# Forward and backward of two SSM-convolution and MLP layers on one core: order of the loads for the last products, storing of the shift gradient, and the last output block in two column halves

## The chip, the cores and the metric

The kernel runs on 1 core of one Trainium2 chip. The metric is device time in microseconds (us); lower is better. A core has TensorE (PE, whose weight loads the profile lists apart as PEld), VectorE (DVE), ScalarE (ACT), GpSimd (POOL) and SyncE (SP); SP, ACT and POOL also issue DMAs.

## The reference

Four residual blocks are applied to x = A_q [1, 2048, 448] (S = 2048 rows, D = 448 columns): block A, block B, block A, block B, each on the layer norm of its input. The outputs are the result and the gradients of eight inputs for a given `grad_out`.

```python
def _A_ref(q, k, v, shift_k, ssm_k, ssm_D):
    k_shift = sum(k_pad[:, t:t+S, :] * shift_k[:, ks-1-t] for t in range(ks))   # ks = 4
    kv = k_shift * v
    y = irfft(rfft(kv, 2*S) * rfft(ssm_k, 2*S))[:S] + kv * ssm_D   # along S
    return q * y
def _B_ref(x, w1, w2):
    return silu(x @ w1) @ w2                                       # 448 -> 1792 -> 448
x = A_q
for f in (_A_ref, _B_ref, _A_ref, _B_ref):
    x = x + f(_layernorm(x), ...)
```

Two of the outputs matter here. Output 7 is the gradient of `w1` [448, 1792]: a sum over the 2048 rows, and over the two B layers, of (normed input) transposed times (gradient at the 1792 columns). Output 4 is the gradient of `A_shift_k` [448, 4].

## The kernel before, in words

The kernel writes its instructions through a small planner. Each call of `Sched.op` (L168) records an operation with a cost per engine that may run it, a priority, and what it reads and writes. `Sched.plan` (L243) then plays the program with these costs and fixes an order for each engine, which buffer of a ring each tile gets, and, where two engines could do an operation, which one does. A DMA's landing is planned from the table `RATE` (L140): "plain", "turn", "load" (transposing loads) and "rows" (stores in short rows). `behind` holds an operation back until others have been issued; `after` until they are done. `emit` (L338) writes the instructions out in the planned order. So a changed cost or `behind` can change the order on every engine from that place on.

The program has three stages: `Head` (the convolution spectra and the first forward product), `Flow` (16 row tiles, each through all blocks forward and backward), and `Tail` (weight gradients and the gradients of block A). The change is in `Tail`:

- `fft`, `chunk` (L848 to L935) take the gradient of `kv` through the Fourier products.
- `ends` (L959) turns the spectra back (`ps_gkv` L980, `ps_gK` L1002) and makes the gradients of v, k, `ssm_k`, `ssm_D` and `shift_k`. For `shift_k`, columns are taken in bands of 32, four bands to a group `q` (groups 0 to 2 have 128 columns, group 3 has 64). TensorE multiplies the bands (`ps_sk`, L1051) in two halves `h` of 8 row tiles; VectorE's `pick` (L1058) takes the diagonals out, sums them (`gsk`, L1063) and writes four columns of `gskb` (L1065), one row for each of the group's columns. After all four groups, TensorE turns the 16 columns of `gskb` into rows (`row4`, L1071 and L1075, PSUM tile `ps_gs`), ScalarE copies the 1 x 1792 result (`gsr`, L1079), and one POOL DMA stores it (L1080).
- `jobs` (L1082) is called for "w2" and for "w1". A job `p` (7 of them, `NF // 2`) makes 256 of the 1792 rows of a weight gradient: two blocks `u` of 128, each a sum of 32 matmuls 128 x 128 by 128 x 448 (L1172): 16 row tiles `t` for each of two groups `gi`, one per B layer. The stationary operand comes from `jb`, a tile of 128 x 16 x 256 brought for each (p, gi) by `bring` (L1107). In the w1 jobs `jb` is brought by a transposing DMA (L1112) from DRAM (`GH1` for gi = 0, `GH0` for gi = 1); its buffers are three of ring `jb`, and `Minv`'s space for every fourth one. The moving operand of the w1 jobs is `nmov` (L1090): two tiles 128 x 16 x 448, `nm[1]` for gi = 0 and `nm[0]` for gi = 1, each loaded by two plain DMAs of 896 KB (L1095). All these loads are issued by SP, in the order that the planner fixed: both loads of `nm[1]`, the last `jb` of the w2 jobs, the transposing load for (0, 0), both loads of `nm[0]` (which are `behind` that load), the transposing load for (1, 0), then (0, 1), (1, 1) and on.
- The order on TensorE in the first two w1 jobs is laid down by hand (L1157, L1174): job 0 with gi = 0 (32 matmuls), job 1 with gi = 0 (32), job 0 with gi = 1, job 1 with gi = 1. The two blocks of job 1 share one PSUM tile of two banks (`pair`, L1150). The `ps_sk` matmuls of the last `shift_k` groups are placed between them.
- A finished block is copied from PSUM to `dob` (L1188, on ScalarE or VectorE by `_copy`, L90, which shows as L92 or L94). For jobs 0 to 5 an SP transposing DMA (L1191) turns `dob` into `do`, and four POOL DMAs store it (L1208, L1210). For the last job TensorE turns `dob` (`ps_dt`, four transposes of 112 columns to a block, L1197), ScalarE or VectorE copies that into `do` (L1200), and one SP DMA stores it (L1212).

```python
            for i in (1, 0):
                for h in range(2):
                    ...
                    s.op({"SP": 0.4}, lambda e, i=i, hs=hs: nc.sync.dma_start(out=nm[i][:, hs, :], in_=_pm(k.N_d[i][:])[:, hs, :]),
                         ..., behind=k.loads[-1 - i:][:1])
...
            for p, gi, at in ((0, 0, pr), (1, 0, pr + 0.2), (0, 1, pr + 1), (1, 1, pr + 2)):
                bring(p, gi, 0, 16, at)
```

Of the kernel before, what the change touches and what calls it, by code (L numbers as in the profile page):

```python
# [12 lines left out]
FP32 = mybir.dt.float32  # L13
BF16 = mybir.dt.bfloat16
ACT = mybir.ActivationFunctionType
# [5 lines left out]
P = 128  # L21
S = 2048
D = 448
# [4 lines left out]
ND = 4  # L28
# [61 lines left out]
def _copy(nc, eng, out, in_):  # L90
    if eng is nc.scalar:
        nc.scalar.copy(out, in_)  # L92
    else:
        eng.tensor_copy(out, in_)  # L94
# [38 lines left out]
class Sched:  # L133
# [3 lines left out]
    AHEAD = 0.2  # L137
    SHARED = 3.0
    STEP = 20
    RATE = {"plain": 300e3, "turn": 160e3, "load": 190e3, "rows": 220e3}  # L140

    def __init__(self, k, bufs, opener, start):
        self.k = k
# [16 lines left out]
    def at(self, base, *key):  # L160
        return base + NUDGE.get(key, 0.0)
# [188 lines left out]
def _pm(ap2d):  # L350
    return ap2d.rearrange("(p j) d -> p j d", j=J)
# [487 lines left out]
class Tail:  # L839
# [119 lines left out]
    def ends(self, pr):  # L959
# [63 lines left out]
        for g in range(8):  # L1023
# [13 lines left out]

            adds.append(s.op({"DVE": 2.9}, add, r=[x for x in prods], w=[a0, a1, gk], prio=pr + 5))
            s.op({"POOL": 0.6}, lambda e, gk=gk, g=g: nc.gpsimd.dma_start(out=out2[:, 2 * g:2 * g + 2, :], in_=gk[:]), r=[gk], prio=pr + 5, dma=("plain", 230e3))
        gskb = s.vb("P2", "gskb", [P, 4, 4], BF16, "gskb")  # L1040
        prev = []
        for q in range(4):
            nb = 4 if q < 3 else 2
            pd = self.unit([P, 4, 32], FP32, "ps_sk")
            for h in range(2):

                def ms_(e, q=q, h=h, nb=nb, pd=pd):
                    for sl_ in range(8 * h, 8 * h + 8):
                        for b in range(nb):
                            c0 = 32 * (4 * q + b)  # L1050
                            nc.tensor.matmul(pd[32 * b:32 * b + 32, :, :], lhsT=gks[:, sl_, c0:c0 + 32], rhs=kx[:, sl_:sl_ + 4, c0:c0 + 32],  # L1051
                                             start=(sl_ == 0), stop=(sl_ == 15), tile_position=(0, 32 * b))

                prev = [s.op({"PE": 1.1}, ms_, r=[*gs, kx], w=[pd], prio=pr + 4, after=[*prev, adds[2 * q + h]])]
            sel = s.vb("P2", "sel", [P, 4, 32], FP32, "gsel")
            gsk = s.vb("P2", "gsk", [P, 4], FP32, "gsk")

            def pick(e, q=q, nb=nb, pd=pd, sel=sel, gsk=gsk):  # L1058
                for b in range(nb):
                    m = k.ident[32 * b:32 * b + 32, 32 * b:32 * b + 32].unsqueeze(1)  # L1060
                    nc.vector.tensor_tensor(out=sel[32 * b:32 * b + 32], in0=pd[32 * b:32 * b + 32], in1=m.to_broadcast([32, 4, 32]), op=ALU.mult)
                n = 32 * nb
                nc.vector.tensor_reduce(out=gsk[0:n], in_=sel[0:n], axis=mybir.AxisListType.X, op=ALU.add)  # L1063
                for j in range(4):
                    nc.vector.tensor_copy(gskb[0:n, q, j:j + 1], gsk[0:n, 3 - j:4 - j])  # L1065

            s.op({"DVE": 1.5}, pick, r=[pd], w=[sel, gsk, gskb], prio=pr + 4)

        pg = self.unit([1, 4, D], BF16, "ps_gs")

        def row4(e):  # L1071
            for q in range(4):
                n = 128 if q < 3 else 64
                for j in range(4):
                    nc.tensor.transpose(pg[0:1, j, 128 * q:128 * q + n], gskb[0:n, q, j:j + 1], k.ident[0:n, 0:n])  # L1075

        s.op({"PE": 1.0}, row4, r=[gskb], w=[pg], prio=pr + 4)
        gsr = s.vb("P2", "gK", [1, D * 4], BF16, "gsr")
        s.op({"ACT": 1.8}, lambda e: nc.scalar.copy(gsr[:].rearrange("o (d j) -> o j d", j=4), pg[:]), r=[pg], w=[gsr], prio=pr + 4)  # L1079
        s.op({"POOL": 0.6}, lambda e: nc.gpsimd.dma_start(out=k.outs[4].rearrange("(o d) j -> o (d j)", o=1), in_=gsr[:]), r=[gsr], prio=pr + 4, dma=("plain", 5e3))  # L1080

    def jobs(self, which, pr):  # L1082
        nc, s, k = self.nc, self.s, self.k
        if which == "w2":
            gm = s.vb("res", "W1", [P, NT, D], BF16, "gmov")
            gs = [gm.sub() for _ in range(4)]
            gl = [lambda i=i: s.op({"SP": 0.4}, lambda e: nc.sync.dma_start(out=gm[:, 4 * i:4 * i + 4, :], in_=_pm(k.grad_out[0])[:, 4 * i:4 * i + 4, :]), w=[gs[i]], prio=pr - 30, dma=("plain", 458e3), behind=[k.lastA_op]) for i in range(4)]
            groups = [("A1", [gs[t // 4] for t in range(NT)], lambda t: gm[:, t, :]), ("A0", k.G2v, lambda t: k.G2[:, t, :])]
        else:
            nm = [s.vb("PF", ("A1", "B1v")[i], [P, NT, D], BF16, "nmov") for i in range(2)]  # L1090
            nh = [[v.sub() for _ in range(2)] for v in nm]
            for i in (1, 0):
                for h in range(2):
                    hs = slice(8 * h, 8 * h + 8)
                    s.op({"SP": 0.4}, lambda e, i=i, hs=hs: nc.sync.dma_start(out=nm[i][:, hs, :], in_=_pm(k.N_d[i][:])[:, hs, :]),  # L1095
                         r=[k.st_[("n", i, j)] for j in range(8 * h, 8 * h + 8)], w=[nh[i][h]], after=self.done[i], prio=pr - 30 if i else pr + 0.5, dma=("plain", 917e3), behind=k.loads[-1 - i:][:1])
            groups = [("GH1", [nh[1][t // 8] for t in range(NT)], lambda t: nm[1][:, t, :]), ("GH0", [nh[0][t // 8] for t in range(NT)], lambda t: nm[0][:, t, :])]
        out7 = k.outs[7].rearrange("(c p) f -> p c f", p=DC)
        prev = []
# [21 lines left out]
        if which == "w2":  # L1121
            bring(0, 1, 0, 16)
            for x in gl:
                x()
            for a in ((0, 0, 0, 15), (1, 1, 0, 16), (1, 0, 0, 15)):
                bring(*a)
        else:
            for p, gi, at in ((0, 0, pr), (1, 0, pr + 0.2), (0, 1, pr + 1), (1, 1, pr + 2)):
                bring(p, gi, 0, 16, at)
        for p in range(NF // 2):  # L1130
            q = s.at(pr + 12.5 * p, p, which)
            early = p < 2
# [26 lines left out]
            both = True  # L1159
            steps = [(u, gi) for gi in range(2) for u in range(2)] if both else [(u, gi) for u in range(2) for gi in range(2)]  # L1160
            if split is None:
                split = [(u, gi, range(8 * h, 8 * h + 8)) for u, gi in steps for h in range(2)]
            mine = []
            for x, (u, gi, ts) in enumerate(split):
                ends = [[y for y in range(len(split)) if split[y][0] == u][z] for z in (0, -1)]
# [4 lines left out]
                def mm(e, ts=ts, gi=gi, u=u, rows=rows, ps=pss[u], at=groups[gi][2], first=(x == ends[0]), last=(x == ends[1])):  # L1170
                    for t in ts:
                        nc.tensor.matmul(ps[:, :D], lhsT=rows(t, gi, u), rhs=at(t), start=(first and t == ts[0]), stop=(last and t == ts[-1]))  # L1172

                if (which, p, x) == ("w1", 1, 4):  # L1174
                    prev = [first[-1], mine[-1]]
                prev = [s.op({"PE": 0.19 * len(ts)}, mm, r=[*[parts[gi][t] or k.lastA for t in ts], *[groups[gi][1][t] for t in ts]], w=[pss[u]], prio=q + 0.05 * x - (12.35 if (which, p) == ("w1", 1) and x < 4 else 0), after=prev + (self.last if p else [k.lastG] if u and which == "w2" else []))]
# [5 lines left out]
            for u in range(2):  # L1182
                ps = pss[u]
# [4 lines left out]
                s.op({"ACT": 0.55, "DVE": 0.62}, lambda e, ps=ps, ob=ob: _copy(nc, e, ob[:], ps[:, :D]), r=[ps], w=[ob], prio=q)  # L1188
# [4 lines left out]
                pt = self.unit([DC, ND, P], BF16, "ps_dt")  # L1193

                def tr(e, ob=ob, pt=pt):
                    for dc in range(ND):
                        nc.tensor.transpose(pt[:, dc, :], ob[:, dc * DC:(dc + 1) * DC], k.ident[:])  # L1197

                s.op({"PE": 0.25}, tr, r=[ob], w=[pt], prio=q)
                s.op({"ACT": 0.6, "DVE": 0.4}, lambda e, pt=pt, o=o, u=u: _copy(nc, e, o[:, :, u, :], pt[:]), r=[pt], w=[o], prio=q)  # L1200
# [14 lines left out]
def kernel(  # L1215
# [66 lines left out]
               u=3, cp=6, junk=1, cc=6, tt=1, G3=2, gy2=3, G1=1, gy=1, gq=2),  # L1282
    "PF": dict(A1=1, Minv=1, B1v=1, gks=1, kx=1),
    "P1": dict(pq=3, sp=1),
    "P2": dict(skb=1, gK=2, gkv=2, gKD=1, sel=2, gsk=2, gskb=1, gKr=1, oo=2, ob=2),
}


# [98 lines left out]
```

## Time and profile before

| | us |
|---|---|
| median of 3 runs | 701.48 (700.76 to 703.49) |
| the profiled execution: its own time | 699.83 |
| its span, first to last instruction | 698.0 |
| TensorE busy | 676.8 |
| VectorE busy | 512.8 |
| ScalarE busy | 401.8 |
| GpSimd busy | 168.2 |
| first matmul of the w1 jobs, from the span's start | 601.53 |

Times in views are us from the start of the span. Busy matmul times overlap a little, since a matmul's end is modelled with the pipeline behind it; the spacing of matmuls is read from the starts of the runs that follow each other. "x32" is a run of 32 like instructions; what stands in brackets is idle time before it, and what ended it. The DMA view gives, per kind of issue, the count, the size and the time from issue to landing.

### The profile page before, as it was taken

The numbers are of one execution on the slowest core, as the hardware profiler recorded it, in microseconds if no ns is written. First come the engines' busy times: TensorE is split into PE (matmuls) and PEld (weight loads), VectorE is DVE, ScalarE is ACT, GpSimd is POOL, SyncE is SP. The second block draws the span as 40 slices with busy tenths as digits, with TensorE's granted clock in tenths as the row PEclk, the third lists the DMA queues.
The fourth block names the chain that finished last, engine by engine and source line by source line (L and its number), as shares of the span: only waits on it lengthen the run. The fifth ranks groups of instructions, "written<-read, shape, count | busy, mean of one in ns | idle before, by whom it ended". The sixth has DMA issues, their size and how long they took to land. (4 is left out here: it accounts for less than half of the span.)

```text
span 698.0 us, 18012 instructions
## 1 busy us (share of the span) xinstructions
PE 676.8 (97%) x7448; PEld 469.2 (67%) x7464; DVE 512.8 (73%) x1203; ACT 401.8 (58%) x486; POOL 168.2 (24%) x290
## 2 busy tenths in 40 slices
PE   6999898999999999999999999999999999999997
PEld 4887666776767776777767767655767765455553
DVE  5989798668889888888889877864699679951000
ACT  4989987776667556766567666425876550002001
POOL 1254153203222323122212201013143131102221
PEclk9999999999999999999999999999999999999999
DMA  9979988989788978787886769977699679999972
GB/s 320 289 247 291 363 165 181 199 180 190 181 154 180 183 189 181 177 176 187 183 181 143 174 158 237 296 191 231 201 387 350 181 258 302 302 238 219 230 159 46
DMA packets 280671, 151.86 MB, mean 218 GB/s; under 512 B 230159, under 2 KB 261631, under 8 KB 280205
## 3 DMA queue, kind: packets, MB, share of 16 engines
q1 hardware_dynamic: 265854, 108.29, 67.2%
q0 software_dynamic: 13968, 41.62, 19.5%
q8 instruction: 58, 0.95, 0.6%
q10 hardware_dynamic: 766, 0.80, 0.4%
q14 instruction: 25, 0.20, 0.1%
HBM read 50.68 MB, written 54.60 MB: 151 GB/s over the span
## 5 line engine op out<-in xcount | busy, mean ns | idle before, releaser
L1172 PEld LDWEIGHTS <-jb 128*128 128x128 bf16 x892 | 85.8, 98 | 81.6 <-DMA jb<-GH_d 2.0
L92 ACT CAST ghp<-ps_g 128x896 bf16<-128x896 f32 x64 | 58.1, 908 | 58.5 <-PE ps_g L672 48.5
L726 PE MATMUL ps_o<-w2sb,aT 128*128 128x448 bf16 x448 | 89.7, 352 | 0.8 <-ACT aT L700 0.8
L726 PE MATMUL ps_n<-w1T,ghT 128*128 128x448 bf16 x448 | 90.0, 352 | 0.0
L1172 PE MATMUL ps_d<-nmov,jb 128*128 128x448 bf16 x448 | 86.3, 353 | 2.2 <-DMA jb<-GH_d 1.6
L663 PE MATMUL ps_h<-nT,w1sb 128*128 128x128 bf16 x1344 | 85.6, 219 | 0.8 <-ACT nT L92 0.8
L663 PE MATMUL ps_g<-nT,w2T 128*128 128x128 bf16 x1344 | 85.7, 219 | 0.0
L663 PEld LDWEIGHTS <-w2T 128*128 128x128 bf16 x1344 | 77.3, 98 | 7.2
L663 PEld LDWEIGHTS <-w1sb 128*128 128x128 bf16 x1344 | 76.7, 98 | 5.2 <-issue 0.9
L726 PEld LDWEIGHTS <-aT 128*128 128x128 bf16 x448 | 43.0, 98 | 38.4 <-ACT aT L700 1.0
L726 PEld LDWEIGHTS <-ghT 128*128 128x128 bf16 x448 | 43.1, 98 | 37.8
L700 ACT ACTIVATE aT<-ps_h 128x896 bf16<-128x896 f32 x64 | 56.7, 916 | 19.9 <-PE ps_h L672 11.0
L622 POOL TENSOR_TENSOR rstd<-ve,mhalf 128x1 f32<-128x1 f32 x64 | 39.3, 614 | 106.6 <-DVE ve L619 106.6
L700 ACT ACTIVATE dT<-ps_h 128x896 bf16<-128x896 f32 x60 | 53.3, 915 | 14.9 <-PE ps_h L672 10.0
L750 DVE SCALAR_TENSOR_TENSOR junk<-u,n 128x448 bf16<-128x448 bf16 x64 | 39.9, 624 | 23.2 <-ACT u L829 22.2
L92 ACT CAST dob<-ps_d 128x448 bf16<-128x448 f32 x13 | 6.9, 532 | 70.9 <-PE ps_d L1172 70.9
L700 ACT ACT_TABLE_LOAD x36 | 46.2, 1283 | 1.2 <-issue 0.6
L1172 PE MATMUL ps_d<-G,jb 128*128 128x448 bf16 x224 | 45.7, 353 | 0.1
L1172 PE MATMUL ps_d<-gmov,jb 128*128 128x448 bf16 x220 | 45.1, 352 | 0.0
L617 DVE BATCH_NORM_STATS2 st<-x 128x6 f32<-128x448 bf16 x64 | 40.0, 625 | 1.5
L739 DVE TENSOR_TENSOR ghT<-ghp,dT 128x896 bf16<-128x896 bf16 x64 | 39.4, 620 | 1.1 <-ACT ghp L92 0.9
L829 ACT ACTIVATE u<-ps_n,rstd 128x448 bf16<-128x448 f32 x32 | 20.3, 636 | 32.3 <-POOL rstd L622 13.8
(180 smaller groups left out, 1218.2 us busy)
## 6 DMA issues: line engine op xcount, KB each, us to landing
A_d<-turned SPq DMA_DIRECT2D x32, 448.0 KB, 4.0
GH_d<-ghT SPq DMA_DIRECT2D x32, 448.0 KB, 4.1
jb<-A_d SPq DMA_DIRECT2D x12, 1024.0 KB, 6.7
KK<-KK POOLq DMA_DIRECT2D x14, 256.0 KB, 5.1
spec_K<-KK POOLq DMA_DIRECT2D x7, 512.0 KB, 6.0
spec_KV<-X POOLq DMA_DIRECT2D x7, 512.0 KB, 7.7
N_d<-n POOLq DMA_DIRECT2D x32, 112.0 KB, 4.0
sp_c<-spec_KV POOLq DMA_DIRECT2D x14, 256.0 KB, 6.6
```

The costliest lines, as they stand in the source:

```text
L92: nc.scalar.copy(out, in_)
L617: nc.vector.bn_stats(out=st[:], in_=x[:])
L622: s.op({"POOL": 1.0}, lambda e: nc.gpsimd.tensor_tensor(out=rs[:], in0=ve[:], in1=self.k.mhalf[:, 0:1], op=ALU.pow), r=[ve], w=[rs], prio=pr)
L663: nc.tensor.matmul(ps[:, i, :], lhsT=at(b, ft), rhs=nT[:, b, :], **f)
L700: prev = [s.op({"ACT": 0.93}, lambda e, i=i, fun=fun, out=out, late=late: nc.scalar.activation(out[:, 7 * i:7 * i + 7, :], c[:, 7 * i:7 * ...
L726: nc.tensor.matmul(po[:, :D], lhsT=a[:, ft, :], rhs=wt[:, ft * D:(ft + 1) * D], start=(ft == 0), stop=(ft == NF - 1))
L739: s.op({"DVE": 0.57}, lambda e, i=i, t=t: nc.vector.tensor_tensor(out=gh[:, 7 * i:7 * i + 7, :], in0=t[:], in1=d[:, 7 * i:7 * i + 7, :], o ...
L750: nc.vector.scalar_tensor_tensor(out=junk[:], in0=u[:], scalar=1.0, in1=n[:], op0=ALU.mult, op1=ALU.mult, accum_out=cp[:, 1:2])
L829: s.op({"ACT": 0.85}, lambda e: nc.scalar.activation(u[:], pn[:, :D], ACT.Identity, scale=r[:], accum_out=cp[:, 0:1]), r=[pn, r], w=[u, cp ...
L1172: nc.tensor.matmul(ps[:, :D], lhsT=rows(t, gi, u), rhs=at(t), start=(first and t == ts[0]), stop=(last and t == ts[-1]))
```

## The change

Three edits in `Tail`, and one number of the planner:

1. The loads of `nm[0]` move: they are recorded behind the second transposing load, (1, 0), instead of the first, (0, 0).
2. The gradient of `shift_k` is no longer turned on TensorE. Each group `q` has a small tile `gskb` [128, 4] of its own (4 buffers), and one POOL DMA a group stores its 128 (or 64) rows of 4 elements to output 4. `row4`, the copy `gsr` and its store are gone.
3. In the last w1 job block u = 1 is computed in two column halves (224 columns each) with a PSUM tile each; copying, turning and copying out of that block go by halves.
4. `RATE["load"]` goes from 190e3 to 215e3, which the planner uses for the transposing loads only.

On TensorE the built order differs as follows. The 16 `ps_gs` transposes are gone, and 32 matmuls of 448 columns are now 64 of 224. From the first w1 matmul on, the order before is 40 matmuls, 32 `ps_sk`, 32, 32 `ps_sk`, 56, 16 `ps_sk`, 24, 16 `ps_sk`, 16, then `ps_gs`; after, it is 8 matmuls, 32 `ps_sk`, 48, 32 `ps_sk`, 32, 16 `ps_sk`, 24, 16 `ps_sk`, 288. At the end, after the last 16 matmuls of block u = 0: before 8 matmuls, 4 transposes (u = 0), 8 matmuls, 4 transposes; after (the 16 half-width ones of the first half, 4 transposes (u = 0), 8 half-width, 2 transposes, 8 half-width, 2 transposes). On SP the two `nm[0]` loads and the load (1, 0) change places, and three of the later `dob` turns move by one load. Before the w1 jobs the engines' orders are the same but for VectorE's, where in groups 1 and 2 one product and the `pick` change places, and POOL's, which has the four new stores. One `dob` copy of job 2 goes from VectorE to ScalarE.

```diff
-    RATE = {"plain": 300e3, "turn": 160e3, "load": 190e3, "rows": 220e3}
+    RATE = {"plain": 300e3, "turn": 160e3, "load": 215e3, "rows": 220e3}
...
-        gskb = s.vb("P2", "gskb", [P, 4, 4], BF16, "gskb")
...
+            gskb = s.vb("P2", "gskb", [P, 4], BF16, "gskb")
...
-                    nc.vector.tensor_copy(gskb[0:n, q, j:j + 1], gsk[0:n, 3 - j:4 - j])
+                    nc.vector.tensor_copy(gskb[0:n, j:j + 1], gsk[0:n, 3 - j:4 - j])
...
-        pg = self.unit([1, 4, D], BF16, "ps_gs")
-
-        def row4(e):
-            for q in range(4):
-                n = 128 if q < 3 else 64
-                for j in range(4):
-                    nc.tensor.transpose(pg[0:1, j, 128 * q:128 * q + n], gskb[0:n, q, j:j + 1], k.ident[0:n, 0:n])
-
-        s.op({"PE": 1.0}, row4, r=[gskb], w=[pg], prio=pr + 4)
-        gsr = s.vb("P2", "gK", [1, D * 4], BF16, "gsr")
-        s.op({"ACT": 1.8}, lambda e: nc.scalar.copy(gsr[:].rearrange("o (d j) -> o j d", j=4), pg[:]), r=[pg], w=[gsr], prio=pr + 4)
-        s.op({"POOL": 0.6}, lambda e: nc.gpsimd.dma_start(out=k.outs[4].rearrange("(o d) j -> o (d j)", o=1), in_=gsr[:]), r=[gsr], prio=pr + 4, dma=("plain", 5e3))
+            n, lo = (128 if q < 3 else 64), 128 * q
+            s.op({"POOL": 0.6}, lambda e, gskb=gskb, n=n, lo=lo: nc.gpsimd.dma_start(out=k.outs[4][lo:lo + n, :], in_=gskb[0:n, :]), r=[gskb], prio=pr + 4, dma=("rows", 30e3))
...
-            for i in (1, 0):
+
+            def rows_of(i, behind):
                 for h in range(2):
                     hs = slice(8 * h, 8 * h + 8)
...
+            rows_of(1, k.loads[-2:-1])
...
                 bring(p, gi, 0, 16, at)
+                if (p, gi) == (1, 0):
+                    rows_of(0, k.load)
...
+            cols = [(0, 0, D), (1, 0, D)]
+            if (which, p) == ("w1", NF // 2 - 1):
+                cols = [(0, 0, D), (1, 0, D // 2), (1, D // 2, D)]
+                pss.append(self.unit([P, 512], FP32, "ps_d"))
...
-                        nc.tensor.matmul(ps[:, :D], lhsT=rows(t, gi, u), rhs=at(t), start=(first and t == ts[0]), stop=(last and t == ts[-1]))
+                        nc.tensor.matmul(ps[:, c0:c1], lhsT=rows(t, gi, u), rhs=at(t)[:, c0:c1], start=(first and t == ts[0]), stop=(last and t == ts[-1]))
...
+                ds = range(c0 // DC, c1 // DC)
+                pt = self.unit([DC, len(ds), P], BF16, "ps_dt")
...
+                s.op({"ACT": 0.2 + 0.4 * w, "DVE": 0.1 + 0.3 * w}, lambda e, pt=pt, o=o, u=u, ds=ds: _copy(nc, e, o[:, ds[0]:ds[-1] + 1, u, :], pt[:]), r=[pt], w=[o], prio=q)
...
-    "P2": dict(skb=1, gK=2, gkv=2, gKD=1, sel=2, gsk=2, gskb=1, gKr=1, oo=2, ob=2),
+    "P2": dict(skb=1, gK=2, gkv=2, gKD=1, sel=2, gsk=2, gskb=4, gKr=1, oo=2, ob=2),
```

More of the change, by code (lines that the diff above doesn't have):

```diff
@@ L1091, in jobs @@
             nh = [[v.sub() for _ in range(2)] for v in nm]
-            for i in (1, 0):
+            def rows_of(i, behind):
                 for h in range(2):
                     hs = slice(8 * h, 8 * h + 8)
-                    s.op({"SP": 0.4}, lambda e, i=i, hs=hs: nc.sync.dma_start(out=nm[i][:, hs, :], in_=_pm(k.N_d[i][:])[:, hs, :]),
-                         r=[k.st_[("n", i, j)] for j in range(8 * h, 8 * h + 8)], w=[nh[i][h]], after=self.done[i], prio=pr - 30 if i else pr + 0.5, dma=("plain", 917e3), behind=k.loads[-1 - i:][:1])
+                    s.op({"SP": 0.4}, lambda e, hs=hs: nc.sync.dma_start(out=nm[i][:, hs, :], in_=_pm(k.N_d[i][:])[:, hs, :]),
+                         r=[k.st_[("n", i, j)] for j in range(8 * h, 8 * h + 8)], w=[nh[i][h]], after=self.done[i], prio=pr - 30 if i else pr + 0.5, dma=("plain", 917e3), behind=behind)
+            rows_of(1, k.loads[-2:-1])
             groups = [("GH1", [nh[1][t // 8] for t in range(NT)], lambda t: nm[1][:, t, :]), ("GH0", [nh[0][t // 8] for t in range(NT)], lambda t: nm[0][:, t, :])]
@@ L1158, in jobs @@
                 prev = first[:4]
-            both = True
-            steps = [(u, gi) for gi in range(2) for u in range(2)] if both else [(u, gi) for u in range(2) for gi in range(2)]
+            cols = [(0, 0, D), (1, 0, D)]
+            if (which, p) == ("w1", NF // 2 - 1):
+                cols = [(0, 0, D), (1, 0, D // 2), (1, D // 2, D)]
+                pss.append(self.unit([P, 512], FP32, "ps_d"))
             if split is None:
-                split = [(u, gi, range(8 * h, 8 * h + 8)) for u, gi in steps for h in range(2)]
+                split = [(v, gi, range(8 * h, 8 * h + 8)) for gi in range(2) for v in range(len(cols)) for h in range(2)]
@@ L1163, in jobs, with mm @@
             mine = []
-            for x, (u, gi, ts) in enumerate(split):
-                ends = [[y for y in range(len(split)) if split[y][0] == u][z] for z in (0, -1)]
+            for x, (v, gi, ts) in enumerate(split):
+                u, c0, c1 = cols[v]
+                ends = [[y for y in range(len(split)) if split[y][0] == v][z] for z in (0, -1)]
                 def rows(t, gi, u, p=p, early=early, st=st):
                     return k.lastA[:, 2 * p + u, :] if early and which == "w2" and (gi, t) == (0, 15) else st[gi][:, t, u * P:(u + 1) * P]
-                def mm(e, ts=ts, gi=gi, u=u, rows=rows, ps=pss[u], at=groups[gi][2], first=(x == ends[0]), last=(x == ends[1])):
+                def mm(e, ts=ts, gi=gi, u=u, rows=rows, ps=pss[v], c0=c0, c1=c1, at=groups[gi][2], first=(x == ends[0]), last=(x == ends[1])):
@@ L1171, in mm @@
                     for t in ts:
-                        nc.tensor.matmul(ps[:, :D], lhsT=rows(t, gi, u), rhs=at(t), start=(first and t == ts[0]), stop=(last and t == ts[-1]))
+                        nc.tensor.matmul(ps[:, c0:c1], lhsT=rows(t, gi, u), rhs=at(t)[:, c0:c1], start=(first and t == ts[0]), stop=(last and t == ts[-1]))
                 if (which, p, x) == ("w1", 1, 4):
                     prev = [first[-1], mine[-1]]
-                prev = [s.op({"PE": 0.19 * len(ts)}, mm, r=[*[parts[gi][t] or k.lastA for t in ts], *[groups[gi][1][t] for t in ts]], w=[pss[u]], prio=q + 0.05 * x - (12.35 if (which, p) == ("w1", 1) and x < 4 else 0), after=prev + (self.last if p else [k.lastG] if u and which == "w2" else []))]
+                prev = [s.op({"PE": 0.19 * len(ts) * (c1 - c0) / D}, mm, r=[*[parts[gi][t] or k.lastA for t in ts], *[groups[gi][1][t] for t in ts]], w=[pss[v]], prio=q + 0.05 * x - (12.35 if (which, p) == ("w1", 1) and x < 4 else 0), after=prev + (self.last if p else [k.lastG] if u and which == "w2" else []))]
@@ L1181, in jobs @@
                 prev = [first[-1], mine[-1]]
-            for u in range(2):
-                ps = pss[u]
+            for v, (u, c0, c1) in enumerate(cols):
+                ps = pss[v]
                 if which == "w2":
@@ L1187, in jobs @@
                 ob = obs.sub(lambda obs=obs, u=u: obs.t[:, u, :])
-                s.op({"ACT": 0.55, "DVE": 0.62}, lambda e, ps=ps, ob=ob: _copy(nc, e, ob[:], ps[:, :D]), r=[ps], w=[ob], prio=q)
+                w = (c1 - c0) / D
+                s.op({"ACT": 0.14 + 0.41 * w, "DVE": 0.1 + 0.5 * w}, lambda e, ps=ps, ob=ob, c0=c0, c1=c1: _copy(nc, e, ob[:, c0:c1], ps[:, c0:c1]), r=[ps], w=[ob], prio=q)
                 if by_dma:
@@ L1192, in jobs, with tr @@
                     continue
[L1193 to L1200, printed above, removed]
+                ds = range(c0 // DC, c1 // DC)
+                pt = self.unit([DC, len(ds), P], BF16, "ps_dt")
+                def tr(e, ob=ob, pt=pt, ds=ds):
+                    for i, dc in enumerate(ds):
+                        nc.tensor.transpose(pt[:, i, :], ob[:, dc * DC:(dc + 1) * DC], k.ident[:])
+                s.op({"PE": 0.06 * len(ds)}, tr, r=[ob], w=[pt], prio=q)
+                s.op({"ACT": 0.2 + 0.4 * w, "DVE": 0.1 + 0.3 * w}, lambda e, pt=pt, o=o, u=u, ds=ds: _copy(nc, e, o[:, ds[0]:ds[-1] + 1, u, :], pt[:]), r=[pt], w=[o], prio=q)
             if which == "w2":
```

2 lines of the change are left out of this document (1 added, 1 removed).

## The prediction

> **What bounds the kernel now.** First the page: the span and the engines' shares.
>
> ```profile
> span 698.0 us, 18012 instructions
> ...
> PE 676.8 (97%) x7448; PEld 469.2 (67%) x7464; DVE 512.8 (73%) x1203; ACT 401.8 (58%) x486; POOL 168.2 (24%) x290
> ```
>
> TensorE is busy 97% of the span. Everything changed lies behind the first w1 matmul or beside it, so the chain of waits (the work that ended last, followed back) from 601 us on is read next: start, length, what.
>
> ```profile
> 594.54 14.78 DMA jb<-GH_d
> ...
> 609.36 1.69 PE ps_d L1172 x8
> 611.05 0.56 PE ps_sk L1051 x32
> ...
> 618.33 9.20 PE ps_d L1172 x48
> ...
> 627.55 0.54 ACT dob L92
> ...
> 628.14 1.67 PE ps_d L1172 x8
> 629.81 0.55 PE ps_sk L1051 x16
> ...
> 635.56 3.13 PE ps_d L1172 x16
> 638.70 0.96 PE ps_gs L1075 x16
> 639.66 51.56 PE ps_d L1172 x272
> 691.22 0.22 PE ps_dt L1197 x4
> 691.44 1.53 PE ps_d L1172 x8
> ...
> 692.99 0.54 ACT dob L92
> ...
> 694.05 0.42 DVE do L94
> ```
>
> The reader is to see that the chain leaves TensorE's row at three places: for a transposing load that lands at 594.54 + 14.78 = 609.3; for ScalarE's copy out of the PSUM pair, ahead of 628.14; and for the copies behind the last matmul. Everything else is matmuls back to back (272 in 51.56 us: 189.6 ns each). So each us taken off TensorE's row or off these waits is a us of the time, unless a load is then late.
>
> The loads come next: SP's timeline, each issue alone, with its time to landing from the DMA view (both views cut to that issue's window).
>
> ```profile
> 582.27 11.07 SPq L1112 DMA_TRANSPOSE jb<-GH_d  x1
> jb<-GH_d SPq DMA_TRANSPOSE x1, 15.1
> 594.06 0.38 SPq L1095 DMA_DIRECT2D nmov<-N_d  x1
> nmov<-N_d SPq DMA_DIRECT2D x1, 896.0 KB, 9.3
> 605.53 4.68 SPq L1112 DMA_TRANSPOSE jb<-GH_d  x1
> jb<-GH_d SPq DMA_TRANSPOSE x1, 8.6
> ```
>
> Load (0, 0) lands at 582.27 + 15.1 = 597.4, `nm[0]` at 594.06 + 9.3 = 603.4, load (1, 0) at 609.3 (the chain), load (0, 1) at 605.53 + 8.6 = 614.1. They land one behind the other: 6.0, 5.9 and 4.8 us apart. I read that as one queue worked off in order; load (1, 0) is late because 1.8 MB of `nm[0]`, not needed until later, stand ahead of it.
>
> **The change part by part.** The sum is made against the profiled execution, 699.83 us (span 698.0 and 1.83 around it). The median of the runs shown, 701.48, is 1.65 above; I carry the difference over to it.
>
> *Loads.* SP's issue of load (1, 0) moves up to where the first `nm[0]` load stood, behind the end of the first issue at 582.27 + 11.07 = 593.3. The buffer that it waits for is free: it was read last by the G matmuls of w2 job 5, before the gmov run at 588.10.
>
> ```profile
> 588.10 3.19 PE L1172 MATMUL ps_d<-gmov,jb 128*128 128x448 bf16 x16
> 601.53 6.22 PE L1172 MATMUL ps_d<-nmov,jb 128*128 128x448 bf16 x32
> ```
>
> With the spacings above in the new order: (1, 0) lands at 597.4 + about 5 = 602.4, `nm[0]` 6.0 later, 608.4, and (0, 1) 5.9 later, 614.3. TensorE needs them, in its new order from 601.53 on: 8 matmuls (8 x 0.1896 = 1.52), 32 `ps_sk` (0.56), 24 (4.6) put the first use of (1, 0) at 608.2; 24 more (4.6), 32 `ps_sk` (0.56) and 8 (1.52) put the first use of (0, 1) and `nm[0]` at 614.9. The first wait goes, with 5.8 us to spare. Its price: 32 matmuls from 601.53 take 6.1, so the next could start at 607.6 and started at 609.36, and the first 8 took 1.69 instead of 1.51; **1.8 us**. What is late next is (0, 1): 614.3 against 614.9, only 0.6 to spare. The other loads of the stream keep their places; (1, 1) is needed 6.5 us after (0, 1), against a spacing of 5. The three later `dob` turns on SP that move by one load wait for job ends; the load behind each is needed a job (12 us) later.
>
> *Planner's number.* It sets no time on the chip, only the order. In the new order block u = 0 of job 1 ends just ahead of a 16-matmul `ps_sk` run, not 8 matmuls ahead of its copy. The copy of the pair, which held TensorE from where its run would have ended (48 matmuls from 618.33 take 9.1: 627.4) to 628.14, 0.75 us, now lies beside that run (0.55): **0.55 us** gained, 0.2 left. The `ps_sk` run reads `gks` and `kx`, long on the chip, so it is good cover; without it the 0.55 come back.
>
> *Shift gradient.* TensorE loses `ps_gs`: 0.96 on the chain, and the 16 matmuls ahead took 3.13 where 16 x 0.1896 = 3.03: **1.05 us**. ScalarE's copy of one partition goes too; it is hidden, as ScalarE is idle there between `dob` copies. Added are three more POOL issues, beside a GpSimd that is busy 24%; behind them in its queue stand gradient stores that nobody waits for before the end.
>
> The nearest row to the new stores, in the view of its source line, the last line from issue to landing:
>
> ```profile
> L388 ACTq DMA_DIRECT2D skb<-in_A_shift_k_dram x1: 422/422/422, 0.7 to 0.7; - x1
> DMA to landing us min/median/max: 4.1/4.1/4.1
> ```
>
> The stores move 8 bytes a piece, 128 pieces. That row loads the same tensor, 448 such pieces, in 4.1 us to landing, so at most 4.1 x 128/448 = 1.2 us of the shared DMA each, and at least nothing; two of them stand ahead of load (0, 1). I take 0.2 for both, which puts (0, 1) at 614.5 and leaves 0.4 to spare, since the row's 4.1 holds the fixed latency too.
>
> *Last block.* Behind the last matmul ScalarE copies 224 columns instead of 448, TensorE turns 2 blocks instead of 4, and the copy out has 256 elements instead of 512, now on ScalarE.
>
> ```profile
> L92 ACT CAST ghp<-ps_g 128x896 bf16<-128x896 f32 x64 | 58.1, 908 | 58.5 <-PE ps_g L672 48.5
> L92 ACT COPY do<-ps_dt 112x512 bf16<-112x512 bf16 x1 | 0.6, 591 | 0.0
> ```
>
> ```profile
> 528.05 0.22 PE L924 MATMUL ps_v<-Gsb,pq 128*128 128x128 bf16 x1
> ...
> 528.78 0.22 PE L925 MATMUL ps_v<-Gsb,pq 128*128 128x128 bf16 x1
> ```
>
> ScalarE goes from 0.54 (448 columns) to 0.91 (896), 0.84 ns a column: 224 columns save 0.19, and the copy out is an estimated 0.59 - 0.21 = 0.38 against VectorE's 0.42. Two transposes fewer save 0.11. So 0.35 behind the last matmul. Ahead of it, `ps_v` matmuls of 128 columns, each with a weight load of its own, start 56 ns apart (TensorE's timeline: 14 starts, the last 0.73 us behind the first); between that and 189.6 at 448 columns, 224 columns cost about 96 ns, 64 of them 0.1 us more than 32 whole ones, and two transposes move ahead (0.11; four took 0.22). **0.1 us** gained; bounds -0.3 and +0.35. The first half's copy (0.34) and turn lie beside 8 half matmuls (0.8).
> On this the Trainium skill, "TensorE: Matmul & The Clock Gate", section "Back-to-back issue gap", speaks against the change: it gives a sustained spacing of about 81 ns at 128 columns and 131 at 512. By a line between these, 64 at 224 columns would cost an estimated 2.1 us more than 32 at 448, and the sum below would be 1.5, not 3.5. The trace's rows (56 and 189.6 ns) agree with neither of its figures.
>
> The sum: 1.8 + 0.55 + 1.05 + 0.1 = **3.5 us**; 699.83 becomes 696.3, and 701.48 becomes **698.0**.
>
> **The rivals.**
> *A. The wait moves to load (0, 1).* For it: 0.6 to spare in a queue whose spacings vary between 4.8 and 6.0, and the small stores. Against: the bytes ahead of (0, 1) are the same as before, when it landed at 614.1. With two spacings at 6.0 instead of 5 and 5.9 and the stores at their bound of 2.4, it lands at 597.4 + 6 + 6 + 6 + 2.4 = 617.8, 2.9 late; the middle is a wait of 1 to 1.5: 699.3.
> *B. Slower: the issue of load (1, 0) keeps SP for 11 us,* as that of (0, 0) did, and `nm[0]` is then issued at 604.4 and lands, by its 9.3 and 0.6, at 614.3; (0, 1), 5.9 behind it, lands at 620.2, 5.3 late. Less the 3.5, that is +1.8: 703.3. It decides from a landing of (0, 1) at 618.4 on. For it: 11.07 is what that issue took. Against: that one had an `nm[1]` and a `jb` load ahead of it, and the issue at 605.53, behind a transposing load alone, took 4.68.
> *C. The change does not do what it says:* all DMA is saturated, (1, 0) lands no earlier than 609 though it is issued first. Then the 1.8 stay: 699.8.
> *D. Weight loads bound the half-width matmuls:* 32 more loads, bare.
>
> ```profile
> L1172 PEld LDWEIGHTS <-jb 128*128 128x128 bf16 x892 | 85.8, 98 | 81.6 <-DMA jb<-GH_d 2.0
> ```
>
> 32 x 98 ns = 3.1 us: 701.1. Against it: `ps_v` goes at 56 ns with loads just as long, so they overlap. The skill's section named above is a milder form of this.
>
> **How the numbers follow.** Forecast 0.6, A 0.22, B 0.06, C 0.07, D 0.05. The likeliest is 698.0. The range: the forecast spreads by 0.7 on either side (the runs before spread from 700.76 to 703.49, and the terms are good to some 0.4); A and C reach to 700.2. So 697.0 to 700.3, which leaves out B, D and the ends. 0.5% of 701.48 is 3.5 us, about what a measurement of this kernel can tell from no change: the forecast lies on that bound. Half of the forecast's chance and a tenth of A and C's fall beyond it, and 0.08 is for a load wait that is longer in the runs of 701.5 than in the profiled one: faster 0.41; within 0.54; slower 0.05, B with a later landing still.
>
> **What would show it.** In the changed profile: no wait of TensorE on `jb` near 608; load (1, 0) landing near 602, with an issue of about 5 us, and `nm[0]` near 608; load (0, 1) landing at 614 to 615 and a wait there under 0.5; the wait for ScalarE's copy in job 1 near 0.2; no `ps_gs`; half-width matmuls some 96 ns apart; from the last matmul to SP's store 0.35 less. The forecast is wrong if (0, 1) lands past 616, if the issue of (1, 0) takes 11 us, or if the `ps_sk` run no longer covers the copy.

## The result and the profile after

The changed kernel takes **709.58 us** (median of 6 runs, 707.29 to 711.37) where the kernel before takes 701.24 in the runs beside it: ratio 1.0117, 95% interval 1.0092 to 1.0141. It is slower by 8.3 us; the prediction was 698.0. The profiled execution took 709.78 us, with a span of 708.0 (before: 699.83 and 698.0).

First TensorE's waits from 555 us on (engine, line, tile, what was waited for: us in total, times, longest).

```profile
PE ps_d L1170 <- DMA jb<-GH_d: 11.0, 3, 10.4
PE ps_dt L1197 <- ACT dob L92: 0.4, 1, 0.4
```

Before, the line for the loads was this:

```profile
PE ps_d L1172 <- DMA jb<-GH_d: 1.6, 1, 1.6
```

The longest wait for a transposing load, 1.6 us before, is now 10.4. The chain of waits says for which load, and what became of the rest:

```profile
594.30 32.65 DMA jb<-GH_d x2
626.96 0.05 issue
627.00 6.32 PE ps_d L1170 x24
633.32 0.55 PE ps_sk L1050 x16
633.88 4.66 PE ps_d L1170 x24
...
638.56 0.54 ACT dob L92
...
639.14 62.27 PE ps_d L1170 x352
701.41 0.22 PE ps_dt L1197 x4
701.63 0.77 PE ps_d L1170 x8
702.40 0.11 PE ps_dt L1197 x2
702.51 0.78 PE ps_d L1170 x8
...
703.32 0.35 ACT dob L92
...
703.71 0.33 PE ps_dt L1197 x2
...
704.07 0.37 ACT do L92
```

Two loads follow one another in it, (1, 0) issued at 594.30 and (0, 1), which lands at 594.30 + 32.65 = 626.96, 12.5 us past the forecast of 614.5. The second thing to see is that the first 24 matmuls behind the wait take 6.32 us and the next 24 take 4.66. TensorE's timeline and a table of stretches (us; busy time and count of PE, PEld, DVE, ACT and POOL; granted clock, DMA share, GB/s) show the same place:

```profile
602.67 1.69 PE L1170 MATMUL ps_d<-nmov,jb 128*128 128x448 bf16 x8 [0.46 <-DMA jb<-GH_d]
...
609.75 4.71 PE L1170 MATMUL ps_d<-nmov,jb 128*128 128x448 bf16 x24 [0.18 <-DMA jb<-GH_d]
...
627.00 6.32 PE L1170 MATMUL ps_d<-nmov,jb 128*128 128x448 bf16 x24 [10.36 <-DMA jb<-GH_d]
```

```profile
597.00:600.50 3.50, 3.50 (x49) 1.98 (x49) 3.43 (x9) 0.53 (x1) 0.54 (x1) 1.00 1.61 58
...
617.00:627.00 10.00, 0.00 (x0) 0.00 (x1) 8.83 (x11) 0.00 (x0) 1.62 (x3) 0.65 1.13 140
627.00:634.00 7.00, 7.00 (x41) 3.28 (x42) 0.00 (x0) 0.53 (x1) 0.00 (x0) 0.76 1.18 277
```

In this wait TensorE's granted clock falls to a mean of 0.65, and it is 0.76 in the 7 us behind: 6.32 - 4.66 = 1.66 us more. So the time is accounted for. My sum for the profiled execution was 696.3; add the wait of 10.36, the slow matmuls behind it 1.66, the two small waits 0.46 and 0.18, and a first w1 matmul that would have started 0.7 later than in before even without its wait (602.67 - 0.46 against 601.53): 709.7, and 709.78 was measured. The terms for the pair's copy, the turns and the last block came out. The two small waits are for loads that are late too: the first for (0, 0), issued at 582.79 and landed 19.8 us later, at 602.6 (597.4 in before); the second for (1, 0), here in SyncE's timeline and the DMA view:

```profile
594.30 9.12 SPq L1105 DMA_TRANSPOSE jb<-GH_d  x1
jb<-GH_d SPq DMA_TRANSPOSE x1, 15.4
```

It lands at 594.30 + 15.4 = 609.7, no earlier than in before, where the forecast had 602.4. What is left to explain is why these loads, and (0, 1) above all, were late.

The line 597 to 600.5 holds the first hint: the DMA engines show a share of 1.61 and move 58 GB/s, where 594 to 597 us has 1.25 at 297 GB/s. It lies in the landing time of the first small store, which GpSimd issued at 589.03. The view of that source line:

```profile
L1070 POOL DMA_DIRECT2D out_dram<-gskb x4: 538/540/552, 589.0 to 640.7; - x4
...
DMA to landing us min/median/max: 7.0/8.8/10.7
```

The first of them lands 10.7 us after its issue, at 599.7. A store of 1 KB takes 7 to 11 us to land.

### The profile page after: what moved, and what is told of

The parts are those of the page before. It is cut to its first block, busy times and chain, and to the rows that moved or that the text cites. A ratio compares the mean times of both kernels' runs of the same rounds, so it can differ in the third digit from the quotient of the medians.

```text
span 708.0 us, 18064 instructions
## 1 busy us (share of the span) xinstructions
PE 679.9 (96%) x7480; PEld 472.3 (67%) x7480; DVE 512.3 (72%) x1202; ACT 398.6 (56%) x488; POOL 169.9 (24%) x293
## 5 line engine op out<-in xcount | busy, mean ns | idle before, releaser
L1170 PEld LDWEIGHTS <-jb 128*128 128x128 bf16 x924 | 89.3, 98 | 89.5 <-DMA jb<-GH_d 12.3
L1170 PE MATMUL ps_d<-nmov,jb 128*128 128x448 bf16 (+1 forms) x480 | 87.9, 344 | 11.1 <-DMA jb<-GH_d 11.0
L92 ACT CAST dob<-ps_d 128x448 bf16<-128x448 f32 (+1 forms) x15 | 7.6, 507 | 92.1 <-PE ps_d L1170 92.1
```

The lines of the kernel that those rows point to most:

```text
L1170: nc.tensor.matmul(ps[:, c0:c1], lhsT=rows(t, gi, u), rhs=at(t)[:, c0:c1], start=(first and t == ts[0]), stop=(last and t == ts[-1]))
```

## The experiments

Two theories stood at first. **S**: the small stores hold up the transfers beside them. **O**: the new order of SyncE's issues does it by itself. The runs made from the changed kernel by its stores alone have its orders on TensorE and SyncE; where the order of the loads alone is changed, forward from the kernel before or back from the changed one, the planner also moves `ps_sk` runs among the first w1 matmuls.

### The small stores late

The four stores are kept back until the sixth of the seven w1 jobs (the expectation calls it the last); all else is the changed kernel.

```diff
-            s.op({"POOL": 0.6}, lambda e, gskb=gskb, n=n, lo=lo: nc.gpsimd.dma_start(out=k.outs[4][lo:lo + n, :], ...), ...)
+            self.held.append(lambda after, ...: s.op({"POOL": 0.6}, ..., after=after))
...
+            if (which, p) == ("w1", 5):
+                for h in self.held:
+                    h([mine[3]])
```

> The changed kernel with its four 8-byte-a-row stores issued late: GpSimd issues them in the last w1 job, when every load has landed; TensorE's and SyncE's orders are those of the changed kernel. Theory S (the small stores hold up the transfers beside them): load (0, 1) lands near 614 instead of 627, TensorE's wait on it falls from 10.4 us to under 1, and the time is 698 to 699, 3 under before. Rival O (the new order of SyncE's issues alone makes (0, 1) late): the load still lands past 624, the wait stays at 9 to 11 us, and the time is 708 to 710. X (both are needed): a wait between, and 702 to 705.

Measured: 701.02 us (12 runs, 696.77 to 703.42), ratio to before 0.9993 [0.9971, 1.0014]. The chain and the waits of the profiled run, one of the long ones (703.42):

```profile
602.19 18.15 DMA jb<-GH_d
620.34 0.05 issue
620.39 6.40 PE ps_d L1171 x24
```

```profile
PE ps_d L1171 <- DMA jb<-GH_d: 3.5, 1, 3.5
```

Moving 3.5 KB of stores takes 709.58 - 701.02 = 8.6 us off: S holds, and O falls as the cause of the whole loss. But the time is not the 698 to 699 of S: a wait of 3.5 us on (0, 1) stays, and the 24 matmuls behind it are slow again (6.40). A second cause is at work.

### The turns and the single store back

```diff
+        gskb = s.vb("P2", "gskb", [P, 4, 4], BF16, "gskb")
...
+        s.op({"PE": 1.0}, row4, r=[gskb], w=[pg], prio=pr + 4)
+        s.op({"ACT": 1.8}, lambda e: nc.scalar.copy(gsr[:]..., pg[:]), r=[pg], w=[gsr], prio=pr + 4)
+        s.op({"POOL": 0.6}, lambda e: nc.gpsimd.dma_start(out=k.outs[4]..., in_=gsr[:]), r=[gsr], ...)
```

> The changed kernel with the shift gradient turned by TensorE into one row and stored by one DMA, as before; order of loads, planner's number and the last block in halves as changed. S: no wait on (0, 1) over 1 us, and 1.05 us for the turns on TensorE is back: 699 to 700. O: wait of 9 to 11 us, 709 to 711.

Measured: 701.51 us (12 runs, 698.07 to 705.12), ratio 1.0004 [0.9981, 1.0027]; the profiled run, one of the short ones (698.79), has a wait of 0.8 us on (0, 1). Between the two theories, as in the run above: S for most of it, and something that keeps (0, 1) late.

### The order of the loads alone, on the kernel before

```diff
-            for i in (1, 0):
+            rows_of(1, k.loads[-2:-1])
...
+                if (p, gi) == (1, 0):
+                    rows_of(0, k.load)
```

> The kernel before with only the order of the loads changed. S: (1, 0) lands near 602, the wait of 1.8 us near 608 goes and none over 1 us takes its place: 699 to 700 where before has 701.2. O: (0, 1) lands past 624 and the time is 708 to 711.

Measured: 703.41 us (12 runs, 699.65 to 706.1), ratio 1.0035 [1.0012, 1.0057]. Neither theory's number: the order alone costs 2.7 us (0.8 to 4.0 by the interval). The wait near 608 is gone, as forecast, and one of 2.8 has come in its place, on (0, 1), in a profiled run (700.16) that is 3.2 us under the median:

```profile
600.10 16.24 DMA jb<-GH_d
616.34 0.05 issue
```

Up to 0.56 us of this is not the loads': the planner put 32 `ps_sk` behind that wait that stand ahead of it in the changed kernel.

### The small stores alone, on the kernel before

Only the part of the diff on `gskb`, with the loads in their old order and the last block whole.

> The kernel before with only the shift gradient's four small stores in place of the turns and the one store. S: the loads behind the stores land 5 to 10 us later than in before, and TensorE waits for one of them: 704 to 709. O: the loads land where they did in before, the turns' 1 us is saved: 700 to 700.5. X: landings late by 5 us but within the slack, 700 to 702.

Measured: 709.11 us (4 runs, 705.46 to 710.66), ratio 1.0106 [1.007, 1.0142]. By themselves the stores cost 8.4 us more than they save by the medians, 7.4 by the ratio: S, at the upper end of its number. The load that is late is now (1, 0):

```profile
595.34 22.46 DMA jb<-GH_d
617.80 0.05 issue
617.85 3.11 PE ps_d L1162 x8
```

22.46 us to landing, where the same load at the same place took 14.78 before. How much the DMA loses is read from the DMA view, cut to 585 to 628 us (packets, bytes, mean rate), first of before, then of this run, of the changed kernel and of the one with its stores late:

```profile
DMA packets 28605, 11.55 MB, mean 269 GB/s; under 512 B 25845, under 2 KB 27925, under 8 KB 28601
```

```profile
DMA packets 20332, 9.68 MB, mean 225 GB/s; under 512 B 17548, under 2 KB 19628, under 8 KB 20328
```

```profile
DMA packets 17896, 9.05 MB, mean 211 GB/s; under 512 B 15102, under 2 KB 17182, under 8 KB 17891
```

```profile
DMA packets 23423, 10.98 MB, mean 255 GB/s; under 512 B 20541, under 2 KB 22621, under 8 KB 23419
```

In one and the same stretch 1.9 MB less move with the stores than without in both pairs (11.55 to 9.68, 10.98 to 9.05). At 269 GB/s that is 7 us of the shared DMA for the two small stores that lie in the stretch in the first pair and the three in the second: an estimated 2.4 to 3.5 us each (the same reckoning gives 1.4 for the three that go end to end to a scratch tensor, below: 9.88 MB for 10.98).

### The old order, with the stores late

```diff
-            rows_of(1, k.loads[-2:-1])
+            for i in (1, 0):
...
-                if (p, gi) == (1, 0):
-                    rows_of(0, k.load)
```

> The changed kernel with its small stores late and with the order of loads of before (rows for the w1 jobs ahead of the second transposing load): what is left of the change is the turns taken off TensorE, the planner's number and the last block in halves. The runs so far put the new order at no gain; with the old one back, load (1, 0) lands near 609 and the wait of 1 to 2 us on it is back, none on (0, 1) takes its place, and the time is that of before less 1.05 for the turns, 0.55 for the copy and 0.1: 698.5 to 699.5 where before has 700.7. If the order did help and the held stores ate its gain, the time is 700.5 to 702 instead.

Measured: **697.56 us** (5 runs, 697.26 to 698.21) beside 700.93, ratio **0.9950 [0.9936, 0.9963]**: faster than both kernels, and it leaves nothing out. It is also 1 us under the 698.5 to 699.5 expected.

```profile
595.21 14.70 DMA jb<-GH_d
609.91 0.05 issue
609.96 4.71 PE ps_d L1166 x24
```

```profile
PE ps_d L1166 <- DMA jb<-GH_d: 0.9, 1, 0.9
```

(1, 0) lands at 609.9, as before, yet TensorE waits 0.9 us instead of 1.6: the planner, with its new number, puts 32 `ps_sk` (0.56 us) between the 32 matmuls of (0, 0) and the first of (1, 0), ahead of that wait. With the turns (1.05), the copy (0.55) and the end (0.1), these 0.7 make 2.4 us; the two profiled executions are 699.83 - 697.76 = 2.1 apart. The medians are 3.4 apart, so about 1 us has no row: the profiled run of before is one of its shorter ones, and the longer ones were not profiled. That 3.4 is nearly the 3.5 that I had for the whole change is chance, since the order of the loads, which was to bring 1.8 of it, is not in it.

### Three large stores left out

Why does (0, 1) come late in the new order? **P**: three stores of 224 KB that GpSimd issues at 605.8 to 611.1 share the DMA with it. **Q**: a transposing load right behind two large loads is slow in any company. From the kernel with the late stores, with parts of outputs 2 and 8 left unwritten:

```diff
-            s.op({"POOL": 0.6}, lambda e, gk=gk, g=g: nc.gpsimd.dma_start(out=out2[...], in_=gk[:]), ...)
+            if g not in (4, 5):
+                s.op({"POOL": 0.6}, lambda e, gk=gk, g=g: nc.gpsimd.dma_start(out=out2[...], in_=gk[:]), ...)
...
-            if which == "w2":
+            if which == "w2" and p == NF // 2 - 1:
+                pass
+            elif which == "w2":
```

> The changed kernel with its small stores late, and three 224 KB stores left out: two of output 2 (groups 4 and 5) and the last of output 8, which in that run GpSimd issued at 605.8, 606.3 and 611.1, while load (0, 1) was in flight. Theory P (in the new order these stores and the load share the DMA, since the rows for the w1 jobs, ahead of the load, had kept them waiting): (0, 1) lands 5 to 6.5 us behind the last rows, near 614 to 615, the wait falls under 1 us, 697 to 698. Rival Q (a transposing load that SyncE issues right behind two large loads is slow whatever runs beside it): it lands 8 to 11 us behind the rows as in the runs with the new order, the wait stays at 1 to 3.5 us, 699 to 701.

Measured: 696.92 us (4 runs, 696.09 to 697.25), ratio 0.9938 [0.9924, 0.9951]. P's number, about 0.1 us under its range. No wait for a load is left, and in the DMA view, cut to the issue of (0, 1), beside SyncE's timeline there:

```profile
jb<-GH_d SPq DMA_TRANSPOSE x1, 12.6
```

```profile
601.08 8.53 SPq L1107 DMA_TRANSPOSE jb<-GH_d  x1
```

It lands at 601.08 + 12.6 = 613.7. The rows ahead of it (issued at 600.61, 7.5 us to landing) land at 608.1, so it is 5.6 behind them, where I had 5.9. With the three stores the same kernel has the rows at 601.73 + 7.4 = 609.1 and (0, 1) at 620.34, 11.2 behind. The DMA view from 605.7 to 611.2 of that kernel shows the stores' side of it:

```profile
out_dram<-gkp POOLq DMA_DIRECT2D x2, 224.0 KB, 9.8
out_dram<-do POOLq DMA_DIRECT2D x1, 224.0 KB, 11.5
```

They take 9 to 11.5 us and land in the last 4 us ahead of the load. In before the same three are issued at 602.56, 604.10 and 609.38 and take 4.5 to 5.6; the DMA view from 602.5 to 609.4 us:

```profile
out_dram<-gkp POOLq DMA_DIRECT2D x2, 224.0 KB, 4.7
out_dram<-do POOLq DMA_DIRECT2D x1, 224.0 KB, 5.6
```

So the stores lie beside the loads in before too, where (0, 1) lands at 614.1. Leaving them out takes the wait away, which is all that P's run shows. Why they cost more once (0, 1) is issued ahead of them, right behind the rows, is not shown.

### What it is about the small stores

Four runs of the changed kernel with its four stores sent to a scratch tensor (output 4 is left unwritten in them), with the pieces at a distance:

```diff
+    k.far = dram.tile([D, 256], BF16, name="far")
...
-out=k.outs[4][lo:lo + n, :], in_=gskb[0:n, :]
+out=k.far[lo:lo + n, 0:4], in_=gskb[0:n, :]
```

The other three have `[D, 32]`, `[D, 16]` and `[D, 4]` for the scratch tensor: rows 64, 32 and 8 bytes apart. A fifth stores whole rows of 512 bytes, `k.far[lo:lo + n, :]`, from `gks[0:n, 0, 0:256]`; these wait for no `pick` and go out some 3 us earlier or more (from 586.4 us).

Rows 512 bytes apart:

> The changed kernel with its four small stores sent to rows of a scratch tensor 512 bytes apart, 8 bytes to each row as before (output 4 is left unwritten). Theory N (what costs is that pieces share lines of the memory, so that writes of several engines wait for one another): the loads beside the stores run at their usual pace, (0, 1) lands near 614 to 620, 698 to 702. Rival M (what costs is a piece of 8 bytes, wherever it goes): landings and time as in the changed kernel, (0, 1) past 624, 707 to 711.

Rows of 512 bytes, whole:

> The same stores at the same places with 512 bytes to each row of the scratch tensor instead of 8, taken from another tile (output 4 is left unwritten): 64 times the bytes, 64 KB a store. N and M alike: no stall, since pieces are whole; 64 KB cost under 0.3 us at 290 GB/s, (0, 1) lands near 614 to 620, 698 to 702. If it is as slow as the changed kernel (707 to 711), neither holds: then it is the number of pieces, or the queue of GpSimd, and not their size.

Rows of 8 bytes, end to end:

> The control to the stores 512 bytes apart: the same four small stores to a scratch tensor whose rows are 8 bytes, end to end as in output 4 (which is left unwritten). Theory N (pieces that lie end to end in memory hold up the DMA): as slow as the changed kernel, stall of some 3 us in the DMA's rate beside each store, (0, 1) past 624, 707 to 711. Rival T (it is the output tensor itself, not where the pieces lie): as with the pieces apart, 698 to 703.

Rows 64 bytes apart:

> The small stores to rows of a scratch tensor 64 bytes apart, 8 bytes to a row (output 4 is left unwritten). If what pieces must not share is a line of 64 bytes or less: no stall, (0, 1) lands near 617 to 620, 698 to 702. If it is a block of 512 bytes: eight pieces still share one, a stall, and 704 to 710.

Rows 32 bytes apart:

> The same with rows 32 bytes apart. If pieces must not share 64 bytes: two share a line, half a stall or less beside each store, 700 to 706; if 32 bytes are enough: 698 to 702; if a block of 512 bytes counts: 704 to 710.

| pieces | time, us | ratio to before | TensorE's wait on (0, 1), profiled run |
|---|---|---|---|
| 8 bytes, end to end (output 4) | 709.58 | 1.0117 [1.0092, 1.0141] | 10.4 |
| 8 bytes, end to end (scratch) | 707.63 | 1.0096 [1.0062, 1.0130] | 7.4 |
| 8 bytes, 32 apart | 701.31 | 1.0010 [0.9998, 1.0023] | 1.4 |
| 8 bytes, 64 apart | 701.15 | 0.9997 [0.9979, 1.0016] | 3.2 |
| 8 bytes, 512 apart | 701.05 | 0.9992 [0.9976, 1.0007] | 2.9 |
| 512 bytes, end to end | 701.90 | 1.0002 [0.9987, 1.0016] | 3.9 |
| stores late | 701.02 | 0.9993 [0.9971, 1.0014] | 3.5 |

The bytes moved from 585 to 628 us, end to end in scratch, 32 apart and 512 apart:

```profile
DMA packets 21984, 9.88 MB, mean 230 GB/s; under 512 B 19220, under 2 KB 21300, under 8 KB 21979
```

```profile
DMA packets 27296, 10.96 MB, mean 255 GB/s; under 512 B 24641, under 2 KB 26650, under 8 KB 27291
```

```profile
DMA packets 24246, 10.92 MB, mean 254 GB/s; under 512 B 21405, under 2 KB 23485, under 8 KB 24241
```

The profiled run with rows 32 bytes apart is the fastest of its nine (697.07), so its wait of 1.4 does not stand for the median. With the rows end to end in scratch, (0, 1) landed at 622.6, not past 624 as expected; the time fell into the range.

It is neither the count of pieces, nor their size alone, nor the tensor, nor GpSimd's queue: the same 8 bytes 32 bytes apart cost the same as no store in the way. What costs is pieces that lie end to end, four to every 32 bytes. N holds as to where the pieces lie, and the distance that decides is between 8 and 32 bytes; half a stall at 32 was not seen. Rows 16 apart were not run, and a store end to end also lies in 1 KB where 32 apart it lies in 4 KB, so that it is the sharing of 32 bytes that counts is not shown. That writes of several engines wait for one another is N's reading of it, and no run shows it.
The Trainium skill, "DMA: Bandwidth & Descriptors", section "Specifications", says that a transfer needs at least 512 bytes for the full rate and that smaller ones are read, modified and written. By that rule the pieces 32 to 512 bytes apart should have been as bad as those end to end; the runs do not show it (701.1 to 701.3 against 707.6). The Trainium skill, "Collectives: The Full Stack", section "Rules for kernel authors", asks for buffers of collectives to be aligned to 32 bytes, which prevents a read-modify-write; a deciding distance between 8 and 32 bytes agrees with it, though the runs show only the distance, and no record of what the memory does.

## Why the prediction was wrong

**The step that failed: the price of the small stores** ("at most 4.1 x 128/448 = 1.2 us of the shared DMA each ... I take 0.2 for both"). Each costs an estimated 2.4 to 3.5 us of the shared DMA (1.4 in scratch), up to three times what I called a bound, and keeping them back is worth 8.6 us. The bound came from a *load* of 448 pieces of 8 bytes; the row showed reading such pieces end to end and said nothing on writing them. I had filed it under "nearest row" without asking in what a store differs. For pieces 32 bytes apart even my 0.2 would have been near the truth.

**The step behind it: the queue reading** (nm[0] "6.0 later", "(0, 1) 5.9 later, 614.3", "the bytes ahead of (0, 1) are the same as before"). The bytes are nearly the same, GpSimd's three stores among them, but they do not take the same time. From the landing of (0, 0) to that of (0, 1) the DMA view counts 4.73 MB in 16.8 us in before (597.36 to 614.15), 4.79 in 18.3 with the order alone (598.04 to 616.34) and 4.85 in 21.2 with the stores late (599.17 to 620.34). Without the three stores the spacings hold (4.9 from (0, 0) to (1, 0), 4.2, 5.6: (0, 1) at 613.7); with them the last is 8.0 to 11.2. So, apart from the small stores, rival A was what happened: the wait moved to (0, 1), 0.8 to 3.5 us where I gave it 2.9 at most, and it got 0.22. The order of the loads alone is a loss of 2.7 us instead of a gain of 1.8. A landing time read in one order was carried into another; which pairing of transfers costs the difference stays open.

**Rival B** gave the right sign, and its path came out as far as `nm[0]`: SyncE's issue of (1, 0) took 9.1 us, and the second half of `nm[0]`, issued at 604.15, landed 11.1 us later at 615.3 (604.4 and 614.3 in B). But (0, 1) landed 11.7 behind that, not 5.9. With the stores late the issues of (1, 0) and (0, 1) took 5.9 and 10.4 us for 9.1 and 15.5, and 8.5 for (0, 1) without the large ones. So a long issue comes and goes with the stores, as it would if it followed from a slow DMA; that is argued. With the issue of (1, 0) at 5.9 us (0, 1) was late all the same, so the long issue is not needed for it.

**A price left out**: a wait can cost more than its length. Behind the 10.4 us, 1.66 more went in matmuls at a lower clock; behind 3.5 us it was 6.40 - 4.66 = 1.7, and behind 2.9 (rows 512 apart) 6.26 - 4.66 = 1.6. Length alone does not decide it: behind 3.2 us (rows 64 apart) 24 matmuls took 4.71, as behind 0.8 and 0.9, and behind 2.8 (the order alone) 8 took 1.69, as in before. The stretches behind the waits of 3.5 and 3.2 us, granted clock third from the end:

```profile
620.30:627.00 6.70, 6.61 (x34) 3.02 (x36) 5.76 (x8) 0.53 (x1) 1.08 (x2) 0.75 1.21 254
...
619.90:625.20 5.30, 5.28 (x41) 2.80 (x42) 5.26 (x8) 0.53 (x1) 0.54 (x1) 1.00 1.22 277
```

What decides it no run shows. It may be part of why, in runs made beside one another, those with rows 512 apart spread over 4.5 us and those of before over 2.9, while those of 697.56 and 696.92 us, with waits of 0.9 and none, spread over 1.2 at most; only one run of each was profiled, so this is argued, not shown.

**What came out**: load (1, 0) earlier with the order, but only where the small stores were out of the way (602.9 to 605.0, for 602.4), and then no wait for it; no wait for the pair's copy in job 1, which lies beside 16 `ps_sk`; 1.05 us for the turns; 0.35 and 0.37 us for the two copies at the end. Half-width matmuls cost 97 ns each (62.27 + 0.77 + 0.78 = 63.82 us for 304 whole ones at 189.6 and 64 halves, so 6.18 for these), for which I had 96; rival D falls. So does the estimate from the spacing of 81 and 131 ns in the Trainium skill, "TensorE: Matmul & The Clock Gate", section "Back-to-back issue gap". Rival C's landing came true by another cause: in the changed kernel (1, 0), though issued first, lands at 609.7. That the DMA is too full for it to come earlier is not the reason, since it does come earlier once the small stores are late.

Not tried: the new order with the three large stores put off rather than left out, which might gain the 0.6 us between 697.56 and 696.92; the run without them also moves 672 KB less.

## What to carry to other kernels

Price a store by a store: a store of 8-byte pieces end to end held back the transfers beside it for microseconds here, so either turn them into one row on the chip, as the kernel before did, or issue them when no load is due. When a load is moved, redraw the other queues' transfers around it too, since a landing time read in the old order need not hold in the new one, even with the same bytes ahead. And where TensorE's row has a chain without slack, allow for a wait of some 3 us or more to cost more than its length.

## What was not expected of the hardware

- Four stores of 1 KB or less, in pieces of 8 bytes end to end, cost 8.6 us of a 700 us kernel; from 597 to 600.5 us the DMA engines showed a share of 1.61 at 58 GB/s. The same pieces 32 bytes apart cost nothing that could be measured.
- The granted clock of TensorE fell to a mean of 0.65 in an idle stretch of 10 us and stood at 0.76 over the 7 us behind it, where the stretches before and behind show 1.00. In another run a wait of 3.2 us left it at 1.00.
- Three stores of 224 KB on GpSimd's queue put a 1 MB transposing load 5.6 us later, about as long as the load's own spacing, though 672 KB at 269 GB/s are 2.5 us. The same stores landed in 4.5 to 5.6 us in before.
